# Gated attention and GEGLU on one core: keys and queries of the first unit kept in SBUF, another bank order, another place for a weight copy

## The chip, the cores and the metric

The kernel runs on one core of a Trainium2 chip. The engines of the core are TensorE (PE in the profile, its weight loads PEld), VectorE (DVE), ScalarE (ACT), GpSimd (POOL) and SyncE (SP). Each has its own queue of instructions and runs it in order. SP, ACT and POOL also issue DMA transfers, and an engine that has to wait before it issues one holds up everything behind it in its queue. The metric is the device time of one execution in microseconds (us).

## The reference

The input `x` has 2048 tokens of 512 channels. Two branches of it are mixed by a gate for each token:

```python
g = sigmoid((x * gate_w).sum(-1, keepdims=True))
a = attention(x, wqkv) @ wo      # 32 heads of 16 channels
b = (gelu(x @ w_gate) * (x @ w_up)) @ w_down   # 1792 hidden channels
return g * a + (1 - g) * b
```

The attention is local and dilated. Token `s` looks at the eight tokens `s, s-2, ..., s-14`; those before the first token are masked out. All data are float32.

## The kernel before

Tokens are split by parity into two halves (`par` 0 and 1), since a token only attends to tokens of its own parity. In a half, partition `p` holds the eight neighbouring tokens `8p .. 8p+7` when attention runs (`NP = 8`), while the projections leave, for each of eight steps `jj`, one row for each partition.

Every float32 product is made of three passes on TensorE: each operand is split in a high part (rounded to the fast format) and a low part (the rest), and high times high, low times high and high times low are added in PSUM. ScalarE makes the high part by a copy. The low part comes either from a subtraction on VectorE, or from a negated copy on ScalarE and an adding DMA that GpSimd issues.

A half runs in this order. First come the projections: keys and queries of channels 0 to 255 (`cb` 0), then values of all channels with the gate (`cb` 1), then keys and queries of channels 256 to 511 (`cb` 2; `project_one`, spread over the first two stages of the feed-forward part). Then come 14 stages of the feed-forward part, one for each block of 128 hidden channels (`gate_up`). A stage makes seven block products for gate and up, and between them runs four pieces of the down projection of the group of two blocks before (`down`, `pieces`). `idle(0)` to `idle(8)` are the places in a stage where other steps are hung with `at(i, ...)`. The second half does the same and adds the output projection at its end.

Attention runs on VectorE in four units of 128 channels for each half (`scores`, `softmax`, `mix`), as a generator that `pull` advances by a budget. It reads keys, queries and values from DRAM: `take` copies a projection out of PSUM to a staging buffer (tags `hh` and `hl`, six each) and stores it, `load_kq` loads a unit's keys as 15 slots for each partition (seven of the partition before, eight of its own) and its queries as eight. In the first half, SP stores the keys and queries, and ACT's own queue stores the values.

The down weights of block `f` are fetched to a buffer `r` (`fetch_d`, two buffers). `down_w(f)` then makes the low part in its first step (a negated copy on ScalarE, line L433, and the adding DMA on GpSimd, line L434) and the high part in its second (L436). For `f > 1` both steps are hung in stage `f`, at places 4 and 7. `paced` makes an instruction wait for the last matmul that was written before it.

PSUM has eight banks: four in rotation with the tag `p`, and `acc0` to `acc3`. `names` lists the banks of the eight key and query tiles of a half (`cb` 0): the first eight entries for half 0, the next eight for half 1. At the end of half 0, `down` leaves its first four tiles in the `acc` banks and its last four in `p` banks, and ScalarE empties each with line L491.

The order in which instructions stand in each queue is not the order of the source. The framework's scheduler runs a simulated timeline (`schedule_with_timeline_sim=True`) and picks, on each engine, the ready instruction with the best priority. Attention's instructions get a priority 150 places later than where they are written.

Of the kernel before, what the change touches and what calls it, by code (L numbers as in the profile page):

```python
# [10 lines left out]
F32 = mybir.dt.float32  # L11
F32R = mybir.dt.float32r
AF = mybir.ActivationFunctionType
# [3 lines left out]
P = 128  # L17
S, D, F = 2048, 512, 1792
H, DH, W = 32, 16, 8
NT = S // P  # L20
NP = NT // 2
KC = D // P
FC = F // P
CU = 16 * DH
# [3 lines left out]
UC = 128  # L28
# [15 lines left out]
def tile_gated_mix(ctx: ExitStack, tc: tile.TileContext, xt, wqkv, wff, wo, out):  # L44
    nc = tc.nc
    ctx.enter_context(nc.allow_non_contiguous_dma(reason="rows of 512 bytes"))
    pool = ctx.enter_context(tc.tile_pool(name="sb", bufs=1))
# [8 lines left out]
    def tl(tag, dt=F32):  # L56
        return pool.tile([P, COLS.get(tag, 512)], dt, name=tag, bufs=BUFS[tag])
# [31 lines left out]
    KS, VS, QS, OS, WS, DS = {}, {}, {}, {}, {}, {}  # L89
# [84 lines left out]
    z = pool.tile([P, 2, NP], F32, name="z")  # L174
    g = pool.tile([P, 2, NP], F32, name="g")
    gc = pool.tile([P, 2, NP], F32, name="gc")
    names = iter(["p", "p", "acc0", "acc1", "p", "p", "acc2", "acc3"] * 99)
    stages = iter(["hh", "hl"] * 99)

    def qkv_mm(ps, par, jj, cb, kcs, c0=0, cn=512):  # L180
        t = slice((jj % BT) * P, (jj % BT + 1) * P)
        for kc in kcs:
            xh, xl = X[par, jj // BT, kc]
            wh, wl = WC[cb, kc]
            for n, (a, w) in enumerate(((xh, wh), (xl, wh), (xh, wl))):
                LAST[:] = [nc.tensor.matmul(ps[:, :cn], a[:, t], w[:, c0:c0 + cn], start=(kc == 0 and n == 0),  # L186
                                            stop=(kc == KC - 1 and n == 2))]

    def rows(t, jj):
        return t.rearrange("c (p j) d -> j p c d", j=NP)[jj]  # L190

    def take(ps, par, jj, hh, vals, eng=None, tag=None):
        st = tl(tag or next(stages))[:, :512]
        n = CU if vals else 512
        if eng:
            eng.tensor_copy(st[:, :n], ps[:, :n])
        else:
            nc.scalar.activation(st[:, :n], ps[:, :n], AF.Copy)
        two = st.rearrange("p (a c d) -> p a c d", a=2, c=2)
        dst = VS[par, hh] if vals else KS[par, hh]  # L200
        queue = nc.sync if not vals and (hh or not par) else nc.scalar
        queue.dma_start(rows(dst[:, W:], jj), two[:, 0])
        if not vals:
            queue.dma_start(rows(QS[par, hh], jj), two[:, 1])
        elif not hh:
            nc.scalar.activation(z[:, par, jj:jj + 1], ps[:, CU:CU + 1], AF.Copy)
# [23 lines left out]
    def project_one(par, jj):  # L230

        ps = bank(f"acc{jj % BT}")
        qkv_mm(ps, par, jj, 2, range(KC))
        take(ps, par, jj, 1, False, tag=None if jj < 5 else "c")
        pull((2.7, 2.2)[par])
        if jj == NP - 1:
            done.add((par, 2))


    LG = {}  # L240

    def load_kq(par, u):
        hh, c = divmod(u, 2)
        k = pool.tile([P, 2 * NP - 1, UC], F32, name="k")
        q = pool.tile([P, NP, UC], F32, name="q")
        load_slots(k, KS[par, hh][c])
        nc.sync.dma_start(q, QS[par, hh][c].rearrange("(p j) d -> p j d", j=NP))
        LG[par, u] = k, q

    def load_slots(t, src):  # L250
        nc.sync.dma_start(t[:, :NP - 1], src[:S // 2].rearrange("(p j) d -> p j d", j=NP)[:, 1:])
        nc.sync.dma_start(t[:, NP - 1:], src[W:].rearrange("(p j) d -> p j d", j=NP))
# [177 lines left out]
    def down_w(f):  # L430
        d = WD[f] = tl("d", F32R)
        rd = RD.pop(f)
        paced(nc.scalar.activation(d[:, 512:], rd, AF.Copy, scale=-1.0))  # L433
        nc.gpsimd.dma_start(d[:, 512:].bitcast(F32), rd, accum_op=OP.add)  # L434
        yield
        paced(nc.scalar.activation(d[:, :512], rd, AF.Copy))  # L436
# [9 lines left out]
    def copy(ps):  # L446
        s = tl("s")
        nc.scalar.activation(s, ps, AF.Copy)  # L448
        return s
# [15 lines left out]
    def fourth():  # L465
        if late:
            late.pop()()
# [4 lines left out]
    def down(par, gr, t, b):  # L472
        if b == t == gr == 0:
            ACC.update((t, bank(f"acc{t}")) for t in range(BT))
        pp = bank("p") if b else ACC[t]
        if b and gr:
            nc.scalar.activation(pp, RT[BT + t], AF.Copy)  # L477
        ts = slice(t * P, (t + 1) * P)
        for i in range(2):
            hh_, hl_ = Hs[2 * gr + i, b]  # L480
            d = WD[2 * gr + i]
            for n, (a, w) in enumerate(((hh_, d[:, :512]), (hh_, d[:, 512:]), (hl_, d[:, :512]))):
                LAST[:] = [nc.tensor.matmul(pp, a[:, ts], w, start=(i == 0 and n == 0 and gr == 0),  # L483
                                            stop=(i == 1 and n == 2), skip_group_check=True)]
        jj = BT * b + t
        if gr == NG - 1 and par:
            nc.scalar.activation(pp, pp, AF.Copy, scale=gc[:, par, jj:jj + 1])
            ACC[jj] = pp
        elif gr == NG - 1:
            st = tl("s")  # L490
            nc.scalar.activation(st, pp, AF.Copy, scale=gc[:, par, jj:jj + 1])  # L491
            nc.gpsimd.dma_start(out_v[2 * jj], st)
        elif b:
            if gr == 0:
                RT[BT + t] = tl("rt")
            nc.scalar.activation(RT[BT + t], pp, AF.Copy)  # L496
        if par or gr < NG - 2:
            pull(1.2 * PACE[par])
# [75 lines left out]
    def ffn(par):  # L574
        XOP.update(((n, kc), X[par, blk, kc + k]) for n, blk, k in (("a11", 0, 0), ("a12", 0, 2), ("a22", 1, 2))
                   for kc in range(2))
        todo = iter(())
        for f in range(FC):
            do = {}

            def at(i, x, *args):
                do.setdefault(i, []).append(lambda: x(*args))

            if f > 1:
                pieces = [[lambda b=b, i=i: down(par, f // 2 - 1, f % 2 * 2 + i, b)] for b in range(2) for i in range(2)]
            else:
                pieces = [[lambda jj=jj: project_one(par, jj) for jj in jjs]
                          for jjs in (((0, 1), (2, 3), (4,), ()), ((5,), (6,), (7,), ()))[f]]
            if f + 1 < FC:
                for i in range(2):  # L590
                    steps = operands(par, f + 1, i)
                    at(1 + 2 * i, next, steps, None)
                    at(5 + i, next, steps, None)
                at(4 if f != 1 else 8, fetch_d, f + 1)
                for g_ in ((), (0, 1))[f] if f < 2 else (f,):
                    steps = down_w(g_)
                    at(4 if f > 1 else 7, next, steps, None)
                    at(7, next, steps, None)
            else:
                steps = down_w(f)  # L600
                at(1, next, steps, None)
                at(4, next, steps, None)
            if par:
                if f + 2 < FC:
                    at(0, fetch_sums, f + 2)
                else:
                    at(0, fetch_o) if f + 2 == FC else None
                if f + 1 == FC:
                    todo = chain(load_o(), channels_of(0, 0))
                    for i in range(1, 9):  # L610
                        at(i, next, todo, None)
            else:
                if f + 2 < FC:
                    at(1, fetch, f + 2)
                    at(8, combine, f + 2)
                else:
                    at(0, fetch_x, 1, f + 2 - FC)
                if f + 1 < FC:
                    do.setdefault(0, []).insert(0, lambda: keep(f + 1))
                at(0, keep_parts, f)  # L620
                if f + 1 == FC:
                    todo = before()
                    for i in range(2, 9):
                        at(i, next, todo, None)
            gate_up(par, f, pieces, do)
        for _ in todo:
            pass
        fourth()
        if par:
            out_first()  # L630
            oT = {}
        for b in range(2):
            for t in range(BT):
                down(par, NG - 1, t, b)
                if par and t == 0:
                    oT[0, b] = channels(par, 0, b)
                if not par and not b:
                    SPLIT.pop(0)() if t % 2 else again(0, 1 + t)
                elif not par and b:
                    again(1, (2, 3, 0, 1)[t])  # L640
        if par:
            finish(oT)
# [37 lines left out]
    def channels_of(par, half):  # L680

        for u in range(NU):
            need_o(par, u)
            FIRST[u, half] = channels(par, u, half, pair("AS"[half]))
            yield
# [58 lines left out]
    for kc in range(KC):  # L744
# [4 lines left out]
        for blk in range(2):  # L749
            for a, n in first if not blk else ((0, 512),):  # L750
                o = (2 * blk + kc // 2) * 512 + a
# [4 lines left out]
    ps = [bank(next(names)) for _ in range(NP)]  # L756
# [4 lines left out]
        for c in range(2):  # L761
            paced(nc.gpsimd.dma_start(t[c, :W], zero))
    for jj in range(NP):
        take(ps[jj], 0, jj, 0, False, nc.vector if jj % 2 else None)
    done.add((0, 0))
    for kc in range(KC):
        load_cb(1, kc, "c", room)()
# [74 lines left out]
```

## Time and profile before

| | |
|---|---|
| median of 3 runs | 622.79 us (621.55 to 623.01) |
| the profiled execution | 620.25 us, of which its span is 618.5 us |
| TensorE busy | 604.4 us (98% of the span), 2839 matmuls |
| VectorE, ScalarE busy | 512.7 us (83%), 378.8 us (61%) |
| granted TensorE clock | 0.999 |
| DMA | 138.25 MB, mean 224 GB/s |

The spans, waits and chains below are those of the profiled execution. A row of the timeline has the start and the duration in us, the engine (`SPq` and `ACTq` are the queues that issue), the line of the kernel, the operation, what it writes and reads (`out<-in`), the shape and a count; in brackets stands the idle time of the engine before it and what ended that. A view of waits has the waiting instruction, what it waited for, the total in us, how often, and the longest.

### The profile page before, as it was taken

The numbers are of one execution on the slowest core, as the hardware profiler recorded it, in microseconds if no ns is written. First come the engines' busy times: TensorE is split into PE (matmuls) and PEld (weight loads), VectorE is DVE, ScalarE is ACT, GpSimd is POOL, SyncE is SP. The second block draws the span as 40 slices with busy tenths as digits, with TensorE's granted clock in tenths as the row PEclk, the third lists the DMA queues.
The fourth block names the chain that finished last, engine by engine and source line by source line (L and its number), as shares of the span: only waits on it lengthen the run. The fifth ranks groups of instructions, "written<-read, shape, count | busy, mean of one in ns | idle before, by whom it ended". The sixth has DMA issues, their size and how long they took to land.

```text
span 618.5 us, 8213 instructions
## 1 busy us (share of the span) xinstructions
PE 604.4 (98%) x2839; PEld 503.7 (81%) x2839; DVE 512.7 (83%) x594; ACT 378.8 (61%) x629; POOL 81.6 (13%) x109
## 2 busy tenths in 40 slices
PE   8999999999999999999899999999999999999997
PEld 6897778787888887878799888887888888888886
DVE  5915999988998897656779979898898969999882
ACT  5733466767776876756564338357765676684632
POOL 0150011212111211101100002111010111101300
PEclk9999999999999999999999999999999999999999
DMA  8498979999799989785769939877787686947724
GB/s 262 136 291 276 315 229 283 281 278 278 211 299 269 261 243 285 220 215 156 274 193 279 281 90 291 230 198 189 234 200 221 159 263 159 266 116 194 98 62 157
DMA packets 82313, 138.25 MB, mean 224 GB/s; under 512 B 7904, under 2 KB 46944, under 8 KB 82272
## 3 DMA queue, kind: packets, MB, share of 16 engines
q1 hardware_dynamic: 56400, 98.46, 48.3%
q0 software_dynamic: 12672, 32.84, 27.7%
q10 hardware_dynamic: 13200, 6.43, 3.5%
q8 instruction: 22, 0.36, 0.2%
q14 instruction: 19, 0.16, 0.1%
HBM read 68.69 MB, written 41.48 MB: 178 GB/s over the span
## 4 chain that ended last, share of the span: by engine, by line
PE 65%; DMA 16%; issue 10%; DVE 5%; ACT 2%; SPq 1%; POOL 1%; ACTq 0%; POOLq 0%; DVEq 0%
PE p L443 30%; PE acc L483 9%; PE p L483 8%; PE acc L186 8%; PE p L691 5%; DMA d<-r 4%; DMA q<-qs 2%; PE p L186 2%; PE acc L691 2%; DMA r<-wqkv 2%; DMA raw<-wff 1%; DMA v<-vs 1%; DMA r<-wff 1%; DMA raw<-xt 1%; DMA vs<-hh 1%
## 5 line engine op out<-in xcount | busy, mean ns | idle before, releaser
L443 PE MATMUL p<-S,g 128*128 128x512 f32 x672 | 168.4, 389 | 1.0 <-ACT p L518 1.0
L443 PEld LDWEIGHTS p<-S,g 128*128 128x128 f32 x672 | 125.9, 188 | 27.5 <-ACT p L518 1.4
L443 PE MATMUL p<-A,g 128*128 128x512 f32 x504 | 127.4, 391 | 1.7 <-ACT g L411 1.1
L443 PEld LDWEIGHTS p<-A,g 128*128 128x128 f32 x504 | 94.0, 188 | 23.0 <-DVE c L453 2.1
L267 DVE TENSOR_TENSOR prod<-k,q 128x2048 f32<-128x2048 f32 x32 | 73.0, 2281 | 24.5 <-DMA q<-qs 16.3
L407 POOL DMA_DIRECT2D g<-raw x42 | 36.2, 863 | 316.1 <-ACT g L406 209.0
L304 DVE TENSOR_TENSOR prod<-v,lg 128x2048 f32<-128x2048 f32 x32 | 72.9, 2280 | 3.9 <-DMA v<-vs 2.0
L270 DVE TENSOR_REDUCE lg<-prod 128x128 f32<-128x2048 f32 x32 | 73.0, 2281 | 0.2
L483 PE MATMUL p<-d,hh 128*128 128x512 f32 x224 | 68.4, 390 | 0.0
L483 PE MATMUL acc<-d,hh 128*128 128x512 f32 x224 | 61.7, 391 | 2.3 <-DMA d<-r 2.3
L483 PEld LDWEIGHTS acc<-d,hh 128*128 128x128 f32 x224 | 41.7, 188 | 12.5 <-DMA d<-r 3.6
L406 ACT ACTIVATE g<-raw 128x1024 fp32r<-128x1024 f32 (+1 forms) x42 | 41.4, 985 | 15.0 <-DVE raw L388 14.1
L457 DVE TENSOR_TENSOR c<-c 128x512 f32<-128x512 f32 x56 | 38.4, 685 | 14.7 <-ACT c L549 14.4
L483 PEld LDWEIGHTS p<-d,hh 128*128 128x128 f32 x224 | 41.9, 188 | 9.4 <-ACT p L477 0.8
L411 ACT ACTIVATE g<-raw 128x1024 fp32r<-128x1024 f32 (+1 forms) x42 | 41.3, 987 | 12.5 <-PE p L443 12.2
L448 ACT ACTIVATE s<-p 128x512 f32<-128x512 f32 x56 | 33.0, 592 | 25.8 <-PE p L443 25.3
L460 DVE TENSOR_TENSOR hl<-c,hh 128x512 fp32r<-128x512 f32 x56 | 38.2, 682 | 8.4 <-ACT hh L459 8.3
L453 DVE TENSOR_TENSOR c<-p,s 128x512 f32<-128x512 f32 x56 | 38.3, 683 | 7.1 <-PE p L443 4.4
L483 PE MATMUL p<-d,hl 128*128 128x512 f32 x112 | 42.4, 389 | 0.0
L459 ACT ACTIVATE hh<-c 128x512 fp32r<-128x512 f32 x56 | 35.1, 627 | 8.2 <-DVE c L457 7.1
L308 DVE TENSOR_TENSOR prod<-prod 128x1024 f32<-128x1024 f32 x32 | 39.1, 1221 | 0.4
L496 ACT ACTIVATE rt<-p 128x512 f32<-128x512 f32 x48 | 27.9, 591 | 16.6 <-PE p L483 16.4
(136 smaller groups left out, 908.9 us busy)
## 6 DMA issues: line engine op xcount, KB each, us to landing
g<-raw POOLq DMA_DIRECT2D x28, 512.0 KB, 7.1
ws<-g SPq DMA_DIRECT2D x14, 768.0 KB, 5.6
g<-ws SPq DMA_DIRECT2D x14, 768.0 KB, 6.1
raw<-wff SPq DMA_DIRECT2D x28, 256.0 KB, 3.3
r<-wff SPq DMA_DIRECT2D x28, 256.0 KB, 3.9
ws<-raw SPq DMA_DIRECT2D x14, 512.0 KB, 4.8
d<-r POOLq DMA_DIRECT2D x28, 256.0 KB, 5.9
raw<-ws SPq DMA_DIRECT2D x14, 512.0 KB, 4.0
```

What stands on the lines that cost most here:

```text
L186: LAST[:] = [nc.tensor.matmul(ps[:, :cn], a[:, t], w[:, c0:c0 + cn], start=(kc == 0 and n == 0), stop=(kc == KC - 1 and n == 2))]
L267: paced(nc.vector.tensor_tensor(prod, spans(k, jj), q[:, jj:jj + 2, None, :].to_broadcast([P, 2, W, UC]), op=OP.mult))
L270: nc.vector.tensor_reduce(two_of(lg, jj), prod.rearrange("p j w (h d) -> p (j w) h d", d=DH), axis=AX.X, op=OP.add)
L304: paced(nc.vector.tensor_tensor(prod.rearrange("p j w (h d) -> p (j w) h d", d=DH), spans(v, jj).rearrange("p j w (h d) -> p j w h d", d=D ...
L308: nc.vector.tensor_tensor(prod[:, :, :4], prod[:, :, :4], prod[:, :, 4:], op=OP.add)
L406: nc.scalar.activation(lo, raw, AF.Copy, scale=-1.0)
L411: ins = nc.scalar.activation(hi, raw, AF.Copy)
L443: LAST[:] = [nc.tensor.matmul(ps, w_, a_, start=(start and kc == 0 and n == 0), stop=(kc == 1 and n == 2), skip_group_check=True)]
L453: nc.vector.tensor_tensor(c, ps, s, op=OP.add)
L457: nc.vector.tensor_tensor(ge, ge, up, op=OP.mult)
L483: LAST[:] = [nc.tensor.matmul(pp, a[:, ts], w, start=(i == 0 and n == 0 and gr == 0), stop=(i == 1 and n == 2), skip_group_check=True)]
L691: LAST[:] = [nc.tensor.matmul(pa, a, b, start=(first and n == 0), stop=(last and n == 2), skip_group_check=True)]
```

## The change

There are three edits.

Keys and queries of unit 0 of half 0 stay in SBUF. One buffer `kq` of 23 slots replaces the buffers `k` (15) and `q` (8). `take_first` copies each of the first eight PSUM tiles in two instructions: unit 0's keys and queries straight to their slots in `kq`, and those of unit 1 to a staging buffer, from where SP stores them as before. For unit 0, `load_kq` no longer reads DRAM: a memset clears the seven foreign slots of partition 0, and one DMA on SP copies seven slots of partitions 0 to 126 to partitions 1 to 127.

The key and query tiles of half 1 take the banks `acc0` to `acc3` first and then four `p` banks; before, they took two `p`, two `acc`, two `p`, two `acc`.

The first step of `down_w(f)` for `f > 1` is hung at place 2 of the stage and no longer at place 4.

```diff
-    names = iter(["p", "p", "acc0", "acc1", "p", "p", "acc2", "acc3"] * 99)
+    names = iter(["p", "p", "acc0", "acc1", "p", "p", "acc2", "acc3", "acc0", "acc1", "acc2", "acc3", *["p"] * 4])
...
+    KQ = []
+
+    def take_first(ps, jj, copy):
+
+        if not KQ:
+            KQ.append(pool.tile([P, 3 * NP - 1, UC], F32, name="kq"))
+        st = tl(next(stages))[:, :CU].rearrange("p (a d) -> p a d", a=2)
+        two = ps.rearrange("p (a c d) -> p c a d", a=2, c=2)
+        copy(KQ[0][:, NP - 1 + jj::NP], two[:, 0])
+        copy(st, two[:, 1])
+        for a, t in enumerate((KS[0, 0][1, W:], QS[0, 0][1])):
+            nc.sync.dma_start(t.rearrange("(p j) d -> j p d", j=NP)[jj], st[:, a])
...
     def load_kq(par, u):
         hh, c = divmod(u, 2)
-        k = pool.tile([P, 2 * NP - 1, UC], F32, name="k")
-        q = pool.tile([P, NP, UC], F32, name="q")
+        kq = KQ.pop() if KQ else pool.tile([P, 3 * NP - 1, UC], F32, name="kq")
+        k, q = kq[:, :2 * NP - 1], kq[:, 2 * NP - 1:]
+        LG[par, u] = k, q
+        if not (par or u):
+
+            nc.gpsimd.memset(k[:1, :NP - 1], 0.0)
+            nc.sync.dma_start(k[1:, :NP - 1], k[:P - 1, NP:])
+            return
         load_slots(k, KS[par, hh][c])
         nc.sync.dma_start(q, QS[par, hh][c].rearrange("(p j) d -> p j d", j=NP))
-        LG[par, u] = k, q
...
-                    at(4 if f > 1 else 7, next, steps, None)
+                    at(2 if f > 1 else 7, next, steps, None)
                     at(7, next, steps, None)
...
-        take(ps[jj], 0, jj, 0, False, nc.vector if jj % 2 else None)
+        take_first(ps[jj], jj, nc.vector.tensor_copy if jj % 2 else lambda o, i: nc.scalar.activation(o, i, AF.Copy))
```

More of the change, by code (lines that the diff above doesn't have):

```diff
@@ L187, in qkv_mm, with take @@
                                             stop=(kc == KC - 1 and n == 2))]
+    KQ = []
[8 more added lines that the diff above has]
+            nc.sync.dma_start(t.rearrange("(p j) d -> j p d", j=NP)[jj], st[:, a])
     def rows(t, jj):
         return t.rearrange("c (p j) d -> j p c d", j=NP)[jj]
-    def take(ps, par, jj, hh, vals, eng=None, tag=None):
+    def take(ps, par, jj, hh, vals, tag=None):
         st = tl(tag or next(stages))[:, :512]
         n = CU if vals else 512
[L195 to L198, printed above, removed]
+        nc.scalar.activation(st[:, :n], ps[:, :n], AF.Copy)
         two = st.rearrange("p (a c d) -> p a c d", a=2, c=2)
```

## The prediction

> **What bounds the kernel now.** I read the page first, for the share of each engine, then the view of waits of PE, then the timeline around its longest waits.
>
> ```profile
> span 618.5 us, 8213 instructions
> PE 604.4 (98%) x2839; PEld 503.7 (81%) x2839; DVE 512.7 (83%) x594; ACT 378.8 (61%) x629; POOL 81.6 (13%) x109
> ```
>
> ```profile
> PE acc L483 <- DMA d<-r: 2.3, 3, 1.3
> PE p L186 <- ACT s L491: 1.6, 1, 1.6
> ...
> PE acc L186 <- ACT z L206: 1.2, 1, 1.2
> PE p L443 <- ACT g L411: 1.1, 1, 1.1
> ...
> PE p L443 <- ACT p L518: 1.0, 1, 1.0
> ```
>
> TensorE is busy for 98% of the span and idle for 618.5 - 604.4 = 14.1 us, part of which is start and end. No edit takes a matmul away, so a gain can only come out of waits like these five: 7.2 us together. What the edits can lose has no such limit. The first line belongs to the third edit (low parts of the down weights), the second to the bank order; the other three lie in the first 80 us, where the first edit works. The 0.3% that a measurement of this kernel can tell from no change is 1.9 us.
>
> The first 80 us are read from four queues: SP's and ACT's transfers, then VectorE's start of the scores, then TensorE.
>
> ```profile
> 37.88 0.36 SPq L382 DMA_DIRECT2D r<-wff  x1
> 38.67 0.33 SPq L251 DMA_DIRECT2D k<-ks  x1
> ...
> 41.63 0.93 SPq L247 DMA_DIRECT2D q<-qs  x1
> 42.86 0.33 SPq L382 DMA_DIRECT2D r<-wff  x1
> ```
>
> ```profile
> 43.16 0.37 ACTq L202 DMA_DIRECT2D vs<-hl  x1
> ...
> 53.07 0.37 ACTq L202 DMA_DIRECT2D vs<-hl  x1
> 53.48 0.38 ACT L198 ACTIVATE hh<-acc 128x256 f32<-128x256 f32 x1 [2.44 <-PE acc L186]
> ...
> 61.11 1.06 ACT L406 ACTIVATE g<-raw 128x1024 fp32r<-128x1024 f32 x1 [1.36 <-DVE raw L388]
> ...
> 62.07 0.58 ACT L518 ACTIVATE p<-p 128x512 f32<-128x512 f32 x1
> ```
>
> ```profile
> 53.12 2.29 DVE L267 TENSOR_TENSOR prod<-k,q 128x2048 f32<-128x2048 f32 x1 [16.10 <-DMA q<-qs]
> ...
> 60.66 0.42 DVE L388 TENSOR_TENSOR raw<-raw 128x256 f32<-128x256 f32 x1
> ```
>
> ```profile
> 54.75 4.47 PE L186 MATMUL acc<-d,A 128*128 128x512 f32 x19
> ...
> 62.71 0.50 PE L443 MATMUL p<-S,g 128*128 128x512 f32 x1 [0.99 <-ACT p L518]
> ```
>
> One landing, that of the queries at 53.0, releases two chains. VectorE has stood idle for 16.1 us for it; in its queue the combination of weights (L388) stands behind the first scores and ends at 61.08. ScalarE's copy L406 waits for that, L518 stands behind L406, and PE waits for L518 at 62.71. The other chain is ScalarE's own: between 43.16 and 53.07 it issued seven stores of values, and the one at 53.07, the eighth transfer of SP and ACT after the query load at 41.63 (the eighth counts the fetch at 42.86), went out just after that load had landed. Behind it in ScalarE's queue stands the copy at 53.48, which empties a bank for PE's tile at 54.75. I read this as eight transfers in flight for both queues together, the ninth waiting for the oldest.
>
> **Edit 1, the first unit in SBUF.** Removed are three loads of unit 0 (512, 448 and 512 KB) and half of the 16 stores of keys and queries. Added are a memset, which bounds at nothing (POOL has 13% busy), and one copy within SBUF of 127 rows of 7 x 128 x 4 = 3584 bytes, 455 KB. Eight copies out of PSUM become 16.
>
> ```profile
> 28.36 0.60 ACT L198 ACTIVATE hh<-acc 128x512 f32<-128x512 f32 x1 [0.52 <-PE acc L186]
> ...
> 30.48 0.38 ACT L198 ACTIVATE hh<-acc 128x256 f32<-128x256 f32 x1
> ```
>
> ```profile
> 31.71 0.53 PE L186 MATMUL acc<-g,A 128*128 128x258 f32 x3
> ```
>
> A pair of half copies takes 2 x 0.38 = 0.76 us for one of 0.60, so ScalarE's four pairs cost it 0.6 us. The bank that is emptied at 28.36 is written again at 31.71; 2.75 us of PE's work on other banks covers it, and the pairs on VectorE likewise. I take nothing for PE. Without that cover it would be 0.6 us on each engine.
>
> The price of the new copy is what decides.
>
> ```profile
> q1 hardware_dynamic: 56400, 98.46, 48.3%
> ```
>
> ```profile
> k<-ks SPq DMA_DIRECT2D x8, 448.0 KB, 5.3
> ```
>
> The lower bound is the load of the same seven slots on 128 rows: 5.3 us. The upper bound is one DMA engine out of 16: SP's queue moved 98.46 MB in 0.483 x 16 x 618.5 = 4780 us of engine time, 20.6 KB for each us, so 455 KB take 22.1 us. I take the upper one. Every large transfer of this kernel has 128 or 32 rows, which 16 engines share evenly; 127 is prime and can't be shared so. No row shows which of the two holds, and both ends stay in the range.
>
> The Trainium skill (DMA: Bandwidth & Descriptors, in "Why a DMA increments its semaphore by 16 and not by 1") says that a transfer from SP runs on the largest number of engines, up to 16, that divides the slowest dimension of both sides, and names 127 partitions as a case of one engine. No run so far shows this; by it the sum would be the one below, and it speaks against this edit.
>
> The copy needs no landing of the key stores, so it is issued when SP is free after the fetch at 37.88, at about 38.3, and lands at L = 38.3 + 22.1 = 60.4 instead of 53.0. The first scores, L388, L406 and L518 keep their order and follow 7.4 us later, and PE passes the place of 62.71 at 70.1. The other chain agrees: the same value store is still the eighth transfer behind the new copy, the bank comes at 60.9, and PE's tile of 54.75 starts near 62. Behind ScalarE's held queue stand the value copies and the copies of stage 0; PE and then VectorE wait for them. The wait of 1.2 at L206 goes, as the long loads are gone, but PE only reaches the later wait sooner, so nothing comes of it. The wait of 1.1 at L411 hangs on VectorE's softmax, which is late by as much as PE, and stays. **Term 1: +7.4** (bounds: -3.3, if the three early waits go, to +11.6, below).
>
> **Edit 3, low parts sooner.**
>
> ```profile
> 229.60 0.62 ACT L433 ACTIVATE d<-r 128x512 fp32r<-128x512 f32 x1
> ...
> 230.64 0.62 ACT L433 ACTIVATE d<-r 128x512 fp32r<-128x512 f32 x1
> ```
>
> ```profile
> 237.24 0.39 PE L483 MATMUL acc<-d,hh 128*128 128x512 f32 x1
> 238.94 0.73 PE L483 MATMUL acc<-d,hh 128*128 128x512 f32 x2 [1.31 <-DMA d<-r]
> ```
>
> ```profile
> 109.58 0.63 ACT L436 ACTIVATE d<-r 128x512 fp32r<-128x512 f32 x1 [0.49 <-DMA r<-wff]
> ```
>
> The longest of the three waits is at 238.94, for the adding DMA behind the copy at 229.60. Between places 4 and 2 stand two pieces and one product of six matmuls each; at 0.23 us (19 in 4.47 us in the row at 54.75) these 18 are 4.1 us, more than the 1.31 needed. The issue on POOL goes ahead of that for the next block's second group of weights, which is first read in the middle of the next stage; SP's fetch behind it comes sooner. The second such wait goes too. The third, in stage 2, stays for one half: there the fetch of `r` lands only at 109.6, and both copies already follow at once. Of 2.3 I take 2.0, and 0.4 for the restart (238.94 - 237.24 - 0.23 is 1.47, not 1.31). **Term 2: -2.4** (bounds 0 and -2.9).
>
> **Edit 2, the banks.**
>
> ```profile
> 296.38 1.07 PE L483 MATMUL p<-d,hl 128*128 128x512 f32 x4
> 299.10 1.65 PE L186 MATMUL p<-g,A 128*128 128x512 f32 x6 [1.65 <-ACT s L491]
> ```
>
> ```profile
> 297.84 0.63 ACT L169 ACTIVATE d<-r 128x512 fp32r<-128x512 f32 x1 [4.25 <-DMA r<-wqkv]
> 298.38 1.25 ACT L491 ACTIVATE s<-p,gc 128x512 f32<-128x512 f32 x2
> ```
>
> PE waits for a `p` bank that L491 empties at 298.38, since ScalarE was held for 4.25 us by a weight fetch. With four `acc` banks first, two more tiles of 12 matmuls, 5.4 us, stand ahead of the first `p` tile, and they read only what the two `acc` tiles before them have read. The wait is covered: 299.10 - 296.38 - 4 x 0.23 = 1.8. What is late next is the fetch itself, which no matmul of these tiles reads. **Term 3: -1.8** (bounds 0 and -1.9).
>
> **The sum** is +7.4 - 2.4 - 1.8 = +3.2: 620.25 + 3.2 = 623.45 us for a profiled execution. That execution lies 2.54 us under the median of the runs shown (622.79), so the forecast for a median is 626.0. The sign turns where term 1 is 4.2, at a landing of 57.2.
>
> **The rivals.**
>
> *Dealt out.* The new copy runs on many engines, like the 448 KB load in 5.3 us, and lands at 43.6. Scores start 9.4 us sooner, L388 and L406 are done long before PE comes to 62.71, and ScalarE is held by no load: all three early waits go, -3.3. 620.25 - 3.3 - 4.2 = 612.75, on the median 615.3. For it: all transfers shown in the DMA view land in under 10 us. Against it: none of them has an odd number of rows. It decides if the landing is before 57.2. Chance 0.20.
>
> *Late but covered.* The copy is as slow as I say, but the scheduler, which writes the order from simulated times, puts L388 ahead of the scores and the value stores elsewhere, and PE loses 1 us instead of 7.4. 620.25 + 1.0 - 4.2 = 617.05, median 619.6. For it: VectorE has 16.1 us of idle time to fill. Against it: in the trace L388 stood behind scores that were just as late. Chance 0.15.
>
> *Held sooner.* The copy stands further ahead in the queues' order, so that the eighth transfer behind it is an earlier value store. Each store earlier leaves PE one value tile more to do after the landing, 1.4 us (12 matmuls of half width, so half of 12 x 0.23). Three give term 1 = 11.6, and 627.65, median 630.2. For it: the copy needs only what is done by 32 us. Against it: attention's low priority. Chance 0.15.
>
> *Not sooner.* The first step of `down_w` waits for the last matmul written before it, which at place 2 is that of the product carried over from the block before. The row at 230.64 belongs to block 11, yet stands in stage 10, because the piece it waited for ran ahead; now it would come in stage 11. If that happens in even stages too, term 2 is nothing: 625.85, median 628.4. Chance 0.10.
>
> **How the numbers follow.** The forecast has 0.40. Its own range is 623.5 to 628.5, from a landing at 57.9 to 62.9. The range of all cases is 615 to 630: from *dealt out* to *held sooner*. Slower by over 0.3%: 0.31 of the forecast, 0.15 of *held sooner*, 0.08 of *not sooner*, 0.01 of *covered*: 0.55. Faster: 0.19 of *dealt out*, 0.08 of *covered*, 0.01 of the forecast: 0.28. The rest, 0.17, is no change.
>
> **What would show it.** Right: the copy on SP takes about 20 us to land; VectorE's idle time before its first scores reaches to about 60; a value store on ACT goes out only then, and PE has a wait of over 5 us near 54 to 60 that was not there; the lines for L491 and most of `d<-r` are gone from PE's waits. Wrong: a landing before 57, first scores near 44, and no wait of PE between 45 and 80. The sum would be wrong too if a new wait of PE of over 1 us stood behind 300, where no term of mine lies.

## The result and the profile after

| | before | after |
|---|---|---|
| median, beside each other | 622.17 us (621.14 to 623.01) | 640.99 us (639.61 to 644.03) |
| the profiled execution | 620.25 us | 641.92 us |
| its span, granted clock | 618.5 us, 0.999 | 640.1 us, 0.984 |

After takes 1.031 times as long as before (95% interval 1.0266 to 1.0354). The forecast was 626.0 us, with a range of 615 to 630: the direction was right, and the time lies 11 us above the range.

The page of after, span and engines:

```profile
span 640.1 us, 8214 instructions
PE 610.5 (95%) x2839; PEld 507.9 (79%) x2839; DVE 513.2 (80%) x598; ACT 377.7 (59%) x634; POOL 82.4 (13%) x110
```

TensorE is idle for 640.1 - 610.5 = 29.6 us, against 14.1 before. That is 15.5 us of the 21.6 that the span grew. The other 6.1 are busy time, 610.5 against 604.4, for the same 2839 matmuls: they ran slower. The waits of PE in after (what waited, what for, total us, how often, longest) say where it idled:

```profile
PE acc L186 <- ACT z L216: 13.3, 2, 12.0
PE p L498 <- ACT p L492: 2.8, 1, 2.8
PE p L458 <- ACT p L533: 2.1, 1, 2.1
PE p L186 <- ACT rt L85: 2.1, 1, 2.1
PE p L458 <- DVE c L468: 2.0, 1, 2.0
PE p L458 <- DMA g<-raw: 1.9, 2, 1.4
...
PE p L186 <- ACT s L506: 0.5, 1, 0.5
PE acc L498 <- DMA d<-r: 0.2, 1, 0.2
```

(The lines of after have other numbers: L206 of before is L216 here, L443 is L458, L453 is L468, L477 is L492, L483 is L498, L491 is L506, L518 is L533.) One wait of 12.0 us stands above everything. The two lines that the second and third edits were aimed at have shrunk, L491 from 1.6 to 0.5 and `d<-r` from 2.3 to 0.2, and five lines of 1.9 to 2.8 us have come or grown elsewhere.

The timeline of after around the longest wait: SP, ACT, VectorE, PE.

```profile
38.83 0.74 SPq L260 DMA_DIRECT2D kq<-kq  x1
```

```profile
48.10 1.72 ACTq L212 DMA_DIRECT2D vs<-hh  x1
...
66.68 0.37 ACTq L212 DMA_DIRECT2D vs<-hl  x1
67.09 0.38 ACT L208 ACTIVATE hh<-acc 128x256 f32<-128x256 f32 x1 [16.84 <-DMA kq<-kq]
67.37 0.17 ACT L216 ACTIVATE z<-acc 128x1 f32<-128x1 f32 x1
```

```profile
66.69 2.29 DVE L282 TENSOR_TENSOR prod<-kq 128x2048 f32<-128x2048 f32 x1 [27.31 <-DMA kq<-kq]
```

```profile
67.59 6.21 PE L186 MATMUL acc<-d,A 128*128 128x512 f32 x20 [12.01 <-ACT z L216]
...
78.18 1.65 PE L458 MATMUL p<-S,g 128*128 128x512 f32 x6 [2.11 <-ACT p L533]
```

The copy within SBUF is issued at 38.83. VectorE's first scores, which need it, start at 66.69, and ScalarE's store at 66.68 is held until then: ScalarE stands idle for 16.8 us before the copy at 67.09, which is next in its queue. So it landed at 66.6, after 27.8 us. PE's tile at 67.59 needs the bank that ScalarE empties only then. How fast PE ran when it came back is seen in the view of windows (columns: the stretch and its length, then busy us and starts of PE, PEld, DVE, ACT, POOL, then the granted clock, the DMA share and GB/s):

```profile
56.00:66.00 10.00, 0.00 (x0) 0.00 (x0) 0.00 (x0) 0.00 (x0) 0.00 (x0) 0.72 0.37 148
66.00:68.00 2.00, 0.41 (x1) 0.41 (x2) 1.31 (x1) 0.53 (x3) 0.00 (x0) 0.50 0.27 89
68.00:71.00 3.00, 3.00 (x9) 2.34 (x9) 2.97 (x2) 1.23 (x5) 0.00 (x0) 0.57 0.50 149
71.00:76.00 5.00, 5.00 (x23) 3.84 (x21) 4.97 (x4) 0.00 (x0) 0.00 (x0) 1.00 0.53 175
```

Nothing runs on any of the five engines for 10 us, and then the clock is granted at half: 9 matmuls start in 3 us, where later 23 start in 5. The same is seen behind shorter waits later on, here on PE:

```profile
161.25 4.66 PE L458 MATMUL p<-A,g 128*128 128x512 f32 x12 [1.96 <-DVE c L468]
225.10 2.57 PE L458 MATMUL p<-A,g 128*128 128x512 f32 x10 [1.40 <-DMA g<-raw]
302.51 1.10 PE L498 MATMUL p<-d,hh 128*128 128x512 f32 x2 [2.77 <-ACT p L492]
303.41 0.63 PE L498 MATMUL p<-d,hl 128*128 128x512 f32 x1
303.84 3.05 PE L498 MATMUL acc<-d,hh 128*128 128x512 f32 x8
306.73 1.54 PE L458 MATMUL p<-A,g 128*128 128x512 f32 x6
```

At 0.23 us each, the 12 matmuls at 161.25 would take 2.8 us and took 4.66; the 11 from 302.51 to 306.73 would take 2.5 and took 4.22. Behind the wait of 1.40 us nothing of the kind is seen.

With these rows the 21.7 us between the two profiled executions add up. Around the copy: 12.0 of waiting, 1.1 of half clock (ten matmuls in the 3.41 us from 67.59 to 71.00), 1.1 more at L533, 0.1 more at the other wait for `z`, less the wait of 1.1 at L411, which is gone: 13.2. At 161: 2.0 and 1.9. At 225: 1.4. At 302: 2.8 and 1.7. The start of the kernel, which no edit touches, took 2.1 more in this execution: in the first 20 us after starts 79 matmuls at a clock of 0.91, before 88 at 1.00 (below, two windows, the first of after, the second of before); nine matmuls of 0.23 us are 2.1. Of these, 0.5 are a longer wait for `rt` (2.1 for 1.6), the rest is the clock. Less 3.2 for the shrunken waits. The sum is 21.9; small waits are left out of it.

```profile
0.00:20.00 20.00, 16.91 (x79) 13.60 (x80) 13.18 (x26) 12.61 (x20) 1.32 (x6) 0.91 0.74 237
```

```profile
0.00:20.00 20.00, 17.40 (x88) 14.45 (x89) 13.41 (x26) 12.63 (x20) 0.48 (x5) 1.00 0.75 237
```

### The profile page after: what moved, and what is told of

It reads as the page before. It is cut to its first block, busy times and chain, and to the rows that moved or that the text cites. A ratio compares the mean times of both kernels' runs of the same rounds, so it can differ in the third digit from the quotient of the medians.

```text
span 640.1 us, 8214 instructions
## 1 busy us (share of the span) xinstructions
PE 610.5 (95%) x2839; PEld 507.9 (79%) x2839; DVE 513.2 (80%) x598; ACT 377.7 (59%) x634; POOL 82.4 (13%) x110
## 4 chain that ended last, share of the span: by engine, by line
PE 67%; DMA 13%; DVE 10%; issue 5%; ACT 2%; SPq 1%; ACTq 0%; DVEq 0%; POOL 0%; POOLq 0%
PE p L458 32%; PE acc L498 10%; PE p L498 9%; PE acc L186 9%; PE p L706 5%; DMA kq<-kq 4%; DVE lg L285 2%; DVE prod L282 2%; DMA r<-wqkv 2%; PE p L186 2%; PE acc L706 2%; DMA g<-raw 2%; DMA d<-r 1%; DMA v<-vs 1%; DMA r<-wff 1%
## 5 line engine op out<-in xcount | busy, mean ns | idle before, releaser
L458 PE MATMUL p<-S,g 128*128 128x512 f32 x672 | 168.2, 390 | 2.1 <-ACT p L533 2.1
L458 PEld LDWEIGHTS p<-S,g 128*128 128x128 f32 x672 | 126.3, 188 | 28.9 <-ACT p L533 2.5
L458 PE MATMUL p<-A,g 128*128 128x512 f32 x504 | 128.8, 394 | 3.9 <-DVE c L468 2.0
L458 PEld LDWEIGHTS p<-A,g 128*128 128x128 f32 x504 | 94.8, 189 | 25.7 <-DVE c L468 3.5
L282 DVE TENSOR_TENSOR prod<-kq 128x2048 f32<-128x2048 f32 x32 | 73.0, 2280 | 36.9 <-DMA kq<-kq 27.3
L498 PE MATMUL p<-d,hh 128*128 128x512 f32 x224 | 69.3, 391 | 2.8 <-ACT p L492 2.8
L498 PE MATMUL acc<-d,hh 128*128 128x512 f32 x224 | 61.4, 397 | 0.2 <-DMA d<-r 0.2
L449 POOL DMA_DIRECT2D d<-r x28 | 24.1, 861 | 245.6 <-ACT d L448 208.8
L498 PEld LDWEIGHTS p<-d,hh 128*128 128x128 f32 x224 | 42.0, 188 | 11.9 <-ACT p L492 3.2
L498 PEld LDWEIGHTS acc<-d,hh 128*128 128x128 f32 x224 | 42.7, 192 | 10.4 <-ACT d L451 0.7
L186 PE MATMUL acc<-d,A 128*128 128x512 f32 x144 | 36.6, 401 | 12.0 <-ACT z L216 12.0
L468 DVE TENSOR_TENSOR c<-p,s 128x512 f32<-128x512 f32 x56 | 38.2, 684 | 7.9 <-ACT g L426 2.6
L498 PE MATMUL p<-d,hl 128*128 128x512 f32 x112 | 43.3, 391 | 0.0
L186 PEld LDWEIGHTS acc<-d,A 128*128 128x128 f32 x144 | 27.9, 195 | 18.3 <-ACT z L216 12.4
```

The costliest lines, as they stand in the source:

```text
L282: paced(nc.vector.tensor_tensor(prod, spans(k, jj), q[:, jj:jj + 2, None, :].to_broadcast([P, 2, W, UC]), op=OP.mult))
L458: LAST[:] = [nc.tensor.matmul(ps, w_, a_, start=(start and kc == 0 and n == 0), stop=(kc == 1 and n == 2), skip_group_check=True)]
L468: nc.vector.tensor_tensor(c, ps, s, op=OP.add)
```

## The experiments

Ratios are against before on the same chip, with the 95% interval. Medians of before there were 621.73, 622.54, 621.79 and 624.57 us in the four groups below.

### First group: each edit alone, and all three with a copy in two parts

The diffs of the first three are parts of the diff of the change: e1 has all but the lines of `names` and `at(2 ...)`, e2 has the line of `names`, e3 that of `at(2 ...)`.

**e1_first_alone**: the first edit alone, on before. 

> The first edit alone (bank order and the place of the low parts as in the kernel before). Theory, one engine: the copy of 127 rows runs on one DMA engine, lands 25 to 30 us after its issue, holds ScalarE's queue at its eighth transfer behind it and with it TensorE: a wait of 10 to 14 us at L216 near 55, the low parts' waits and the one for L491 (or its line here) still there, 635 to 643 us. Rival, order: the three edits together make a new order of the queues, and that order is the loss: this one alone is within 3 us of the kernel before.

Measured: 635.04 us, 1.0225 (1.0192 to 1.0258). In its profile (633.59 us, 13.3 above before's) the longest wait of PE is the one of after:

```profile
PE acc L186 <- ACT z L216: 11.7, 1, 11.7
```

So the first edit alone carries some 70% of the loss (13.3 of 18.8 us by the medians, taken on two chips).

**e2_banks_alone**: the bank order alone. 

> The second edit alone. One engine: no slow copy, so no long wait; the wait of 1.6 us for L491 near 299 is gone or cut to 0.5, and the time is 0 to 2 us under the kernel before, 620 to 622. Rival, order: the new bank order alone costs over 2 us, with new waits of TensorE between 280 and 350.

Measured: 622.21 us, 1.0017 (0.9988 to 1.0045). Two of the waits of PE, which were 1.6 and 2.3 before:

```profile
PE p L186 <- ACT s L491: 0.2, 1, 0.2
```

```profile
PE acc L483 <- DMA d<-r: 3.1, 3, 1.2
```

The edit does what it says, and no wait of over 0.3 us is left between 285 and 345. But TensorE's idle time over the whole span is 618.1 - 604.8 = 13.3 us, only 0.8 less than before's: what is freed at 299 is in part lost to small waits elsewhere, of which that for `d<-r` (3.1 for 2.3) is the largest.

**e3_low_alone**: the low parts at place 2 alone. 

> The third edit alone. One engine: the two longer waits for the down weights' low parts (238.9 and 268.4) are gone, the one in stage 2 stays, and the time is 1 to 3 us under the kernel before. Rival, order: the adding DMA of the down weights goes ahead of those of the gate and up weights, and new waits for g<-raw or for copies in ScalarE's queue take over: 2 us or more over the kernel before.

Measured: 628.40 us, 1.0117 (1.0058 to 1.0175). The waits of PE:

```profile
PE p L186 <- ACT s L491: 2.4, 1, 2.4
PE p L443 <- DVE c L453: 2.2, 1, 2.2
PE p L443 <- DMA g<-raw: 2.0, 2, 1.1
...
PE acc L483 <- DMA d<-r: 0.3, 1, 0.3
```

The 1 to 3 us of gain did not come, and the rival's 2 us or more over before did. The waits for `d<-r` are gone, as forecast (0.3 for 2.3), and more has come for it, among it 2.0 us for `g<-raw`, which in before is no line of this view. GpSimd's issues in stage 4 show what the moved DMA passed, first in before and then in this kernel:

```profile
137.31 0.86 POOL L407 DMA_DIRECT2D g<-raw  x1 [3.88 <-PE acc L483]
139.36 0.86 POOL L434 DMA_DIRECT2D d<-r  x1 [1.19 <-ACT d L433]
```

```profile
136.53 0.86 POOL L434 DMA_DIRECT2D d<-r  x1 [3.67 <-ACT d L433]
137.48 0.86 POOL L407 DMA_DIRECT2D g<-raw  x1
```

The adding DMA of `d` now goes out ahead of that of `g`. VectorE gets attention's values 2.0 us later, 143.32 (the second row, this kernel) for 141.28 (the first, before), and `c` L453, for which PE waits, stands behind that in its queue:

```profile
141.28 2.29 DVE L304 TENSOR_TENSOR prod<-v,lg 128x2048 f32<-128x2048 f32 x1 [2.01 <-DMA v<-vs]
```

```profile
143.32 2.29 DVE L304 TENSOR_TENSOR prod<-v,lg 128x2048 f32<-128x2048 f32 x1 [3.89 <-DMA v<-vs]
145.53 0.69 DVE L453 TENSOR_TENSOR c<-p,s 128x512 f32<-128x512 f32 x1
```

Most of this delay is there before the moved DMA goes out at 136.53. SP issues the second part of the value load 1.25 us later, at 135.60 for 134.35 (again before first), and its way to landing is 0.8 us longer, 7.7 for 6.9. So at most 0.8 of the 2.0 us can come from the DMA beside it, and what holds SP's issue back is not shown.

```profile
134.35 1.30 SPq L252 DMA_DIRECT2D v<-vs  x1
```

```profile
135.60 0.49 SPq L252 DMA_DIRECT2D v<-vs  x1
```

**e4_two_copies**: all three edits, with the copy cut into 112 and 15 rows.

```diff
-            nc.sync.dma_start(k[1:, :NP - 1], k[:P - 1, NP:])
+            for a, n in ((0, 112), (112, 15)):
+                nc.sync.dma_start(k[1 + a:1 + a + n, :NP - 1], k[a:a + n, NP:])
```

> The changed kernel, with the copy of 127 rows cut in two of 112 and 15 rows, nothing else. One engine: both parts run on many engines, land within 8 us, VectorE's idle time before the first scores falls from 27 us to under 8, the wait of 12 us at L216 is gone with the slow matmuls behind it, and the time is 612 to 626, the upper end if the later waits of the changed kernel stay. Rival, slow path: a copy within SBUF beside this traffic is slow however its rows are cut, the landing stays over 20 us and the time is 638 to 644.

Measured: 623.34 us, 1.0026 (0.9996 to 1.0057). VectorE's first scores start 24.8 us sooner than in after:

```profile
41.90 2.29 DVE L283 TENSOR_TENSOR prod<-kq 128x2048 f32<-128x2048 f32 x1 [4.86 <-DMA kq<-kq]
```

The number of rows of one copy is thus worth 17.7 us (640.99 - 623.34, on different chips; the ratios 1.031 and 1.0026 give the same). But the kernel is still no faster than before.

### Second group: what of a slow copy costs the time

**e5_first_two_copies**: the first edit alone, with the cut of e4. 

> The first edit alone, its copy cut in 112 and 15 rows; bank order and low parts as in the kernel before. One engine: the three early waits for L206, L518 and L411 (3.3 us) go and nothing takes their place, since neither the bank order nor the low parts are touched: 615 to 620. Rival, order: the two PSUM copies for each tile and the earlier scores make new waits, and it is within 2 us of the kernel before or over it.

Measured: 619.73 us, 0.9951 (0.9915 to 0.9987). With a copy that lands soon, the first edit gains about 3 us (0.0049 of 622.54).

**e9_first_banks_two**: e5 and the bank order. 

> The first edit with two copies and the bank order; low parts as before. One engine: 614 to 620, under the kernel with all three edits and two copies by 2 us or more, because the third edit is what costs there. Rival, order: the third edit's loss is particular to its neighbours, and this one is 622 or more.

Measured: 619.58 us, 0.9945 (0.9915 to 0.9976). Beside e5 the bank order adds nothing that can be told from nothing. The comparison with e4, which differs from it by the third edit alone, prices that edit in this company: 3.8 us by the medians, 5.0 by the ratios (0.0081 of 622; the two ran on different chips), and the two intervals do not meet.

**e7_extra_copy**: e5, and behind its two copies a third, of 127 rows, into a buffer that nobody reads before it is overwritten.

```diff
+            sc = pool.tile([P, 2, BT * UC], F32, name="tb").rearrange("p a (j d) -> p (a j) d", d=UC)
+            nc.sync.dma_start(sc[1:, :NP - 1], k[:P - 1, NP:])
```

> As the first edit alone with two copies, and with one more copy of 127 rows to a buffer that nobody reads, issued behind them. It tells the two chains apart. Held queue: the extra copy lands 20 us or more after its issue, ScalarE's value store that is the eighth transfer behind it goes out only then, and TensorE waits 7 to 13 us at L216 though no instruction reads the copy: 627 to 636. Rival, late data: what cost the time in the changed kernel was VectorE waiting for its data; here VectorE starts near 44, and the time is within 2 us of the one without the extra copy.

Measured: 636.21 us, 1.0195 (1.0143 to 1.0247), at the upper end of what was expected for a held queue. The scores start early and the store is held all the same; timeline of VectorE and ACT, and the wait of PE:

```profile
42.20 2.29 DVE L285 TENSOR_TENSOR prod<-kq 128x2048 f32<-128x2048 f32 x1 [5.02 <-DMA kq<-kq]
```

```profile
67.08 0.37 ACTq L212 DMA_DIRECT2D vs<-hh  x1
67.49 0.38 ACT L208 ACTIVATE hl<-acc 128x256 f32<-128x256 f32 x1 [16.49 <-DMA tb<-kq]
```

```profile
PE acc L186 <- ACT hl L208: 11.8, 1, 11.8
```

No one needs this transfer, and it costs 16.5 us over e5, as much as the slow copy itself (e1 is 1.0225, the two intervals overlap). What costs the time is ScalarE's queue, held at a store until an older transfer has landed. That the scores' data come late adds nothing that can be seen.

**e10_row_counts**: transfers within SBUF alone, rows of 3584 bytes, each size twice, each waiting for the one before. 

> A kernel of transfers alone, nothing else is computed: copies within SBUF of 3584 bytes for each row, one after the other, of 128, 127, 126, 125, 124, 120, 113, 112, 64, 61, 32 and 15 rows from SP, each twice, then 128, 127, 113 and 112 rows from POOL. One engine: from SP the counts 127, 113 and 61 take 16 to 22, 14 to 20 and 8 to 11 us, and 128, 126, 120, 112, 64, 32 and 15 take 2 to 4, with 125 and 124 (5 and 4 engines) between at 4 to 8. Rival, slow path: the time goes by the bytes, and 127 lands like 128.

SP's issues in the timeline (of 128, 128, 127 and 127 rows):

```profile
13.00 0.56 SPq L27 DMA_DIRECT2D d<-src  x1
15.81 0.50 SPq L27 DMA_DIRECT2D d<-src  x1
18.55 0.76 SPq L27 DMA_DIRECT2D d<-src  x1
38.94 0.62 SPq L27 DMA_DIRECT2D d<-src  x1
```

128 rows take 15.81 - 13.00 = 2.8 us, and 127 take 38.94 - 18.55 = 20.4. By the same differences 126 rows take 3.6, 125 6.5, 124 9.0, 113 18.4, 112 3.35, 61 11.25 and 15 rows 2.5. Issued from GpSimd, they are not slow (448 and 444.5 KB are 128 and 127 rows; the last column is us to landing):

```profile
d<-src POOLq DMA_DIRECT2D x2, 448.0 KB, 2.8
...
d<-src POOLq DMA_DIRECT2D x2, 444.5 KB, 3.8
```

### Third group: the copy elsewhere, and the third edit by halves

**e6_first_banks_pool**: the first two edits, the copy whole and issued by GpSimd; the diff against e9 is

```diff
-            for a, n in ((0, 112), (112, 15)):
-                nc.sync.dma_start(k[1 + a:1 + a + n, :NP - 1], k[a:a + n, NP:])
+            nc.gpsimd.dma_start(k[1:, :NP - 1], k[:P - 1, NP:])
```

> First edit and bank order as in the changed kernel, low parts as before, and the copy of 127 rows left whole but issued by POOL. One engine, for SP's queue alone: on POOL the transfer alone took 3.8 us, so it lands within 10 us, nothing is held, and the time is within 2 us of the kernel with two copies on SP (616 to 622). Rival, the number of rows is slow on every queue beside other traffic: landing over 20 us and 630 or more.

Measured: 625.26 us, 1.0064 (1.0026 to 1.0101). The copy landed 5.9 us after its issue and held nobody. But the kernel is 1.2% behind e9, with much of the loss in a wait that the copy has no part in:

```profile
PE acc L498 <- DMA d<-r: 6.1, 4, 2.9
```

The landing was foreseen and the time was not (616 to 622). The scheduler wrote another order, and a single order's small waits can cost as much as an edit brings. Why this order has four waits for `d<-r` is not shown.

**e11_low_even** and **e12_low_odd**: e9, with the third edit in even or in odd blocks only.

```diff
-                    at(4 if f > 1 else 7, next, steps, None)
+                    at(2 if f > 1 and f % 2 == 0 else 4 if f > 1 else 7, next, steps, None)
```

> First edit with two copies, bank order, and the third edit in the even blocks alone. Queue theory: what the third edit costs is that the low part's adding DMA goes out ahead of that for the next block's gate and up weights, in every block: 1 to 3 us over the kernel without the third edit, with a wait for g<-raw of over 1 us. Odd theory: the loss comes from the odd blocks, where the new place waits for a later matmul than the old one: 0 to 2 us under the kernel without the third edit, since the two remaining waits for d<-r (1.4 us) go.

> The counterpart: first edit with two copies, bank order, and the third edit in the odd blocks alone. Queue theory: 1 to 3 us over the kernel without the third edit. Odd theory: the whole loss, 3 to 6 us over it. If neither of the two halves loses over 1 us, the loss needs both, and its cause is not in one kind of block.

Measured: even 621.41 us, 1.0012 (0.9986 to 1.0038); odd 617.62 us, 0.9955 (0.9918 to 0.9991). The two stand 3.8 us apart by the medians, though their intervals just touch; against e9 (0.9945, at most 0.9976) the even one is worse and the odd one is not. So the loss shows in the even blocks, and my theory that the odd ones carry it falls. The queue theory does not come out either: it had 1 to 3 us of loss in the odd blocks too, where none is seen, and a wait for `g<-raw` of over 1 us in the even ones, where the profile has 0.5. A wait of PE for `c` of 1.9 to 2.5 us stands in the profiles of all five kernels that have the third edit or a half of it together with its DMA (after, e3, e4, e11, e12), and none of over 1.2 us in the others. But the odd kernel has it too and loses nothing, so this wait alone is not the cause.

### Fourth group: the third edit without its transfer

**e13_no_add_place4** and **e14_no_add_place2**: e9 and e4 with the adding DMA left out, so that only the copy on ScalarE and its place remain.

```diff
-        nc.gpsimd.dma_start(d[:, 512:].bitcast(F32), rd, accum_op=OP.add)
```

> First edit with two copies, bank order, low parts at place 4 as before; the adding DMA of the down weights' low part (28 transfers of 256 KB on POOL's queue) is left out. It is the base for the next one. Transfer theory: the waits for d<-r (1.4 us in the kernel with them) go and the DMA engines have less to do, 613 to 619.

> The same with the low parts at place 2: all three edits with two copies, the adding DMA left out. Transfer theory: what the third edit costs is that this DMA goes out ahead of the next weights' DMA on POOL and beside the load of the values, so without it the place does not matter: within 1.5 us of the one at place 4. Rival, order: the cost is in the place of the copy on ScalarE and in the order that the scheduler makes around it: 2.5 to 5 us over the one at place 4, as with the DMA (3.8 us).

Measured: place 4, 614.03 us, 0.9852 (0.9806 to 0.9898); place 2, 614.53 us, 0.9859 (0.9816 to 0.9903). With the DMA the two places are 3.8 us apart (e4 and e9), without it 0.5. So the loss of the third edit comes with the adding DMA, not with the step's place in ScalarE's queue. Leaving the DMA out also lets the scheduler write another order, so these runs do not say how much of the 3.8 us is the transfer itself and how much the order written around it.

## Why the prediction was wrong in size, and where it was right

**Term 1, the copy: right in its mechanism, too small by about 6 us.** The copy is slow because of its 127 rows, it holds ScalarE's queue, VectorE and PE wait, and a value store goes out just as it lands. All of that is in the rows at 66 to 67. The reading of eight transfers in flight fits, to within one: by the start times the store that is held is the ninth transfer of SP and ACT behind the slow copy in after, e1 and e7, where the first of the nine goes out while the copy's own issue still runs, and it was the eighth behind the load in before. The term that was mis-sized is the landing: 22.1 us after an issue at 38.3, so 60.4. It was issued at 38.83 and landed at 66.6, after 27.8 us. That the scores and all behind them "follow" by as much as the landing is late held: 7.4 and the further 6.2 us of the landing are 13.6, and e1 measured 13.3. The estimate of one engine's rate was not the fault, since alone the copy takes 20.4 us, less than I took.

What was missing is that the copy is not alone in the kernel. The packets in the two traces show where the 7.4 us between 20.4 and 27.8 lie. Both copies are 127 packets of 3584 bytes, of 0.14 us in the median. In e10 they follow one another without gaps and take 18.6 us from the first start to the last end. In after they take 24.2, with 6.3 us of gaps, 4.6 of them between 44.8 and 52.0, while value stores and the next fetch on SP are under way. The other 1.8 us are the start: the first packet comes 3.2 us after the issue, for 1.4 in e10. That packets of the other transfers fill the gaps is inferred, since the records do not say which engine moved a packet. The half clock after the stall, 1.1 us in after, was missing too. The prediction had two chains that "agree", VectorE's and ScalarE's. e7 shows that ScalarE's is enough: with VectorE's data early the loss is the same.

The Trainium skill (DMA: Bandwidth & Descriptors, in "Why a DMA increments its semaphore by 16 and not by 1") named 127 partitions as a case of one engine; the 20.4 us beside 2.8 for 128 rows agree, as do 18.4 and 11.25 for 113 and 61, which are prime too.

**Term 3, the banks: the wait went, the time did not.** L491 fell from 1.6 to 0.2, but -1.8 is outside what e2 allows (1.0017, at least 0.9988, which is -0.7 us). The sentence on what is late next held, since no wait followed up to 345. The step that failed is from "The wait is covered" to a gain of its whole length: waits elsewhere grew, and TensorE's idle time fell by 0.8 us, to 13.3.

**Term 2, the low parts: wrong in sign.** Forecast -2.4; measured +6.7 us by the medians alone (e3) and +3.8 beside the others (e4 and e9). The matmuls between the places did cover the DMA, and the waits for `d<-r` went. The step that failed is the one about the queue it was moved past: "ahead of that for the next block's second group of weights, which is first read in the middle of the next stage". I put nothing for that. The row at 136.53 shows it ahead of a DMA of `g`, and PE's waits for `g<-raw` are 2.0 us in e3 with none in before, and 2.5 in e4 for 0.6 in e9. With the adding DMA gone, the place no longer matters (e13, e14), so the loss comes with that DMA. By which waits it comes stays open: those for `g<-raw` do not tell the even from the odd blocks, and the late values of e3 are late for the most part before the DMA goes out. The rival *not sooner* only let the gain go; I had named no loss from coming sooner.

**The rivals.** *Dealt out* falls with e10. For the copy that is dealt out, e5, its price of -3.3 was good (0.9951 is -3.0 us). *Late but covered* and *held sooner* fall: PE lost 12 us at the very tile of before's 54.75, and the store that was held stands where it stood. *Not sooner* falls, since the `d<-r` waits went. None of the rivals had the case that happened, term 1 nearer to 13 and term 2 positive. Alone, the three edits measured 13.3, 6.7 and 0.5 us, 20.5 together, where all three cost 18.8. Of the 15.0 us by which the forecast was short, about 6 are thus term 1's, and the most of the rest is term 2's.

**What was to show it.** The signs named for "right" came: a landing after about 20 us or more, VectorE idle past 60, a wait of over 5 us near 54 to 60, the lines for L491 and `d<-r` nearly gone. So did the sign named for a wrong sum, a new wait of over 1 us behind 300: the 2.77 at 302.51. What stays open is why one program order has more of these waits than another; no single one of them was settled.

**The better version.** e9, which is after without the third edit and with its copy cut in two, is 0.9945 (0.9915 to 0.9976) of before; e5 (0.9951) and e12 (0.9955) cannot be told from it.

## What to carry to other kernels

A transfer is priced by how its rows divide as much as by its bytes: 127 rows from SP cost seven times what 128 cost, and 112 and 15 rows together cost under a third of it. Ask of each slow transfer not only who reads it but who issues after it, since a store that has nothing to do with it can hold an engine's whole queue until it lands. And when a step with a DMA is moved forward, ask what the DMA now goes ahead of before counting the wait that it removes.

## What the runs showed of the hardware that I had not expected

**A short wait of TensorE can cost 1.7 us more than its length.** In after, waits of 1.96 and 2.77 us were followed by 1.9 and 1.7 us lost at half clock. What is lost does not follow the length of the wait. Behind the wait of 1.96 us the clock was 0.93, 0.50 and 0.71 in the three windows of 2 us from 161 on, which makes 3.4 us of half clock, or 1.7 us lost; here is the second of them:

```profile
163.00:165.00 2.00, 2.00 (x5) 1.63 (x6) 2.00 (x5) 1.12 (x2) 0.00 (x0) 0.50 0.91 302
```

Behind the 2.77 us it was 0.92, 0.50 and 0.73 in the three from 301 on, and behind 2.09 us at the start 0.91 and 0.75 in two windows of 5 us, 3.4 us again each time. In e4 a wait of 1.76 us had the same behind it and one of 2.02 us had not. In e3 a wait of 2.19 us was followed by full clock, 12 matmuls in 3.39 us:

```profile
146.27 3.39 PE L443 MATMUL p<-A,g 128*128 128x512 f32 x12 [2.19 <-DVE c L453]
```

This also goes with the spread of one and the same program. Of the 73 runs of before on which the ratios of the four groups rest, the 46 with a granted clock of 0.999 or 1.000 took 620.9 us in the mean, the 21 at 0.996 or 0.997 took 623.7, and the 6 below that 626.0. And it is a part of the third edit's price: the mean granted clock is 0.9948 in e4 and 0.9987 in e9. A mean lower by 0.0039 is half clock for 0.0078 of 620 us, 4.8 us, which lose 2.4 of the 3.8 us (or of the 5.0 by the ratios); that is an estimate, worked out from these means, and it takes TensorE as busy all that time. The Trainium skill (TensorE: Matmul & The Clock Gate, in "Part 1: The HAM clock gate (the "warmup" mystery)") says that the clock falls to half after about one idle window of 3.4 us, and that the window runs freely. The stall of 12 us agrees. That waits of about 2 us are punished in one place and not in another fits a free window; that waits of 1.96 us are punished at all does not fit 3.4 us, and the measurement decides.

**The same copy is slow from one queue and not from another**: 127 rows took 20.4 us from SP and 3.8 us from GpSimd. The Trainium skill (DMA: Bandwidth & Descriptors, in the section named above) has this as an exception for some direct copies that GpSimd issues, with 127 partitions on all 16 engines; the 3.8 us agree.
